# Dilated local attention and a mixer MLP on one core: the last q/k channels placed by DMA, three blocks turned by DMA, and a new order of all operations

## The chip, the core and the metric

The kernel runs on one core of a Trainium2 chip. The core has five engines that run side by side and meet only at semaphores: PE (matrix multiply, with PEld for its weight loads), DVE (vector), ACT (scalar functions), POOL (general purpose) and SP, which here only issues DMA transfers. Sixteen DMA engines carry them. PE writes its results to PSUM, eight banks of 128 x 512 float32; PE's operands lie in SBUF, 128 partitions wide. The metric is the device time of one execution in microseconds (us), the median of three runs.

## The reference

The input x has 2048 rows of 448 values (bf16). A layer of attention is followed by a mixer and an MLP, each with a residual:

```python
h  = x + A(layernorm(x))            # A: 16 heads of 28, then @ wo
h2 = h + B(layernorm(h))
# A: every query sees 8 keys, at its own row and 2, 4, ... 14 rows before it
off = jnp.arange(8) * 2
logits = einsum("bhsd,bhswd->bhsw", q, k[rows - off]) * 28**-0.5   # masked above the first row
o = einsum("bhsw,bhswd->bhsd", softmax(logits), v[rows - off])
# B: first half mixes rows, second half is an MLP
g  = gelu(layernorm(x) @ w1)        # four groups of 112 channels, moved by +1, -1, +2, -2 rows
x1 = x + moved(g) @ w2
out = x1 + gelu(layernorm(x1) @ w3) @ w4    # 448 -> 1792 -> 448
```

## The kernel before

The rows are worked in four blocks of 512 (block 0 to 3), each of four tiles of 128 rows, through these phases; the names stand in the prediction too.

- N1: statistics of x (DVE) and its normalization, per tile, into `lntm`. A1: the normalized rows are turned so that channels lie on partitions (`transposed`, into `actT`), then the q and k products on PE, in groups of 128 channels: q0, k0, q1, k1, q2, k2, and one group q3k3 of the 64 channels left of each. Each group is copied out of its PSUM bank by ACT or DVE.
- The group q3k3 comes as two half blocks X and Y, with q in partitions 0 to 63 and k in 64 to 127. Four copies of 64x256 put them in place (`qT[..., 3, ...]` and `kr[t]`), and small copies (the halos) fill the 16 rows before each stretch of keys that the attention reaches back to; `kk` holds the other keys, with a halo of its own.
- V: the v product, copied to `vt`; transfers vwp, vwa, vwb and vwc spread `vt` into windows of 80 rows (`vw`).
- A2: attention's logits. DVE multiplies the queries with all eight shifted keys (`qk_r`; qk c0 to c2 are 4096 wide, qk c3 is the half group and 2048 wide), and PE sums over the channels of a head (L c0 to c3). S: the softmax (max, sub, Exp, sum, Ln, Exp, product into `pb`), and its turn on PE, copied out by ACT (pt).
- A3: DVE spreads the weights (bd), PE multiplies them with the windows of v (AV), and ACT or DVE copies the result (aT). O: the product with wo and the residual, which gives h in `xin` (xin sum).
- B1: statistics and normalization of h, a DMA turn, and M: the product with w1, Gelu on ACT into `gT`. Three of the four groups need a second Gelu into moved columns.

The second half runs over five units of 2, 4, 4, 4 and 2 tiles. B2: the mix (the product with w2 of the moved columns; mix2,3 is the pair of tiles 2 and 3) and its residual on DVE (xb); T: normalization and a DMA turn; W3: fourteen groups with w3 and their Gelus; B3: the product with w4, the last sum on DVE (ost) and the store.

A product of two groups is done by `duo`: two matmuls run at a time, one in the upper and one in the lower 64 rows of the array; it has a first and a second half (A and B) that can stand apart in the order.

Nothing of the order is found at run time. `S.add` and `S.group` note every operation with what it reads and writes, numbered as they are made. `ORDER` is a list of these numbers, written out, that gives one sequence for all engines; each engine takes its own operations from it in that order, and waits with semaphores for the others. `arrange` gives out PSUM banks and other buffers along the sequence. `OTHER` lists operations that go to their second engine (mostly ACT to DVE). All DMAs are issued by SP, in the order of the list: a transfer whose data isn't ready holds up all that stand behind it.

`TURN` says for each phase and block how rows are turned: "t" by PE (32 transposes of 64x64 in four groups, two PSUM banks and two copies), "d" by one DMA. `NORM` gives the engine that normalizes ("a": ACT by default, DVE where `OTHER` says so; this needs the negated mean times the inverse deviation, a small operation `nmr` on DVE), `STATS` and `POWER` who makes sums and powers.

Of the kernel before, what the change touches and what calls it, by code (L numbers as in the profile page):

```python
# [5 lines left out]
ACT = mybir.ActivationFunctionType  # L6
# [6 lines left out]
TURN = {'A1': 'tttt', 'B1': 'dddd', 'B2': 'ddddd'}  # L13
NORM = {'N0': 'vvvv', 'N1': 'avvv', 'B1': 'avvv', 'B2': 'avvvv'}
STATS = {'N1': 'vvva', 'B1': 'avaa', 'B2': 'avvvv'}
NBD, NLN, NACT, NSM, NO = 3, 2, 4, 1, 3
POWER = {'N1': 'aaaa', 'B1': 'aaaa', 'B2': 'apapp'}
RESIDUAL = 'ttvv'
ORDER = """
# [30 lines left out]
"""  # L50
OTHER = """
104 127 196 197 199 402 408 411 519 525 528 582 583
# [79 lines left out]
class _Sched:  # L132
# [59 lines left out]
    def arrange(self, sequence, other=()):  # L192
# [4 lines left out]
        done = set()  # L197
        self.gorder = []
        for n, k in enumerate(sequence):
# [3 lines left out]
            op.deps |= op.sdeps  # L203
            for d in op.deps | op.odeps:
                if d not in done:
                    raise RuntimeError("operation %d (%s) stands before %d (%s)" % (k, op.tag, d.idx, d.tag))
# [68 lines left out]
def bass_sequential_preLN__sliding_local_dilated__mixer_s_mlp__prompt_kernel(  # L275
# [25 lines left out]
    A_W4 = A_W + 4 * (1344 + 128)  # L301
    A_QG = A_W4 + NF * 448
# [6 lines left out]
    with ExitStack() as es:  # L309
# [17 lines left out]
        st6 = sb("st6", [128, 8, 6], F32)  # L327
        mv = sb("mv", [128, 3, NTL, 2], F32)
# [20 lines left out]
        P_h3 = _Pool("h3", lambda k: h3T[:, k, :], NF + 2)  # L349
        P_st = _Pool("st", lambda k: st6[:, k, :], 8)  # L350
# [70 lines left out]
        def load_x(i, n):  # L421
            return dma("x%d" % i, xin[:, i:i + n, :], xv[:, i:i + n, :], 128 * n * D * 2)

        def load_rows(chan, dst, src, lo, n):

            for h in range(2):
                dma("%s%s" % (chan, "ab"[h]), dst[:, 2 * h:2 * h + 2, :], src[192 * h:192 * h + 256, lo:lo + n].rearrange("(c k) n -> k c n", k=128), 256 * n * 2)
# [21 lines left out]
        w4_v = B_w4.rearrange("(f k) n -> k f n", k=128)  # L449
        for f in range(0, NF, 7):  # L450
            dma("w4%d" % f, w4_s[:, f:f + 7, :], w4_v[:, f:f + 7, :], 128 * 7 * D * 2)
        for eng in ("sp", "pool", "act"):
            loads = [op for op in S.ops if op.tag == "load" and op.eng == eng]
            for a, b in zip(loads, loads[1:]):
                b.odeps.add(a)
# [164 lines left out]
        def setup_late(after):  # L620
# [18 lines left out]
            late("memset", ap=vw[0:PADK, 0, 0, :], constant=0.0)  # L639
            late("memset", ap=gT[:, :, 0:2], constant=0.0)  # L640
# [31 lines left out]
        def phase_A1(t):  # L672
# [31 lines left out]
            for h, b in enumerate((X, Y)):  # L704
                copy(qT[64 * h:64 * h + 64, 3, now:now + 256], b(lambda v: v[0:64, 0:256]))
                copy(kr[t][64 * h:64 * h + 64, :, PADK:], b(lambda v: v[64:128, 0:256].rearrange("p (j n) -> p j n", j=4)), False)
            copy(kr[t][64:128, :, 0:PADK], last(X, 0, 4), False)
            copy(kr[t][0:64, 1:4, 0:PADK], last(Y, 0, 3), False)
            if t + 1 < NST:
                copy(kr[t + 1][0:64, 0:1, 0:PADK], last(Y, 3, 1), False)  # L710
                copy(kk[t + 1][:, :, 0:PADK], kk[t][:, :, 512:KVW])

        def phase_V(t):
# [3 lines left out]
            def group(il, upper):  # L717
                b = _Tile(P_bank)
                return sums(lambda lo, n: b(lambda v: v[:, 0:D]), lambda c, part: a(lambda v: v[part, il, c, :]),
                            lambda c, part, lo, n: wqkv_s[part, c, 2 * D:3 * D], upper), \  # L720
                    lambda: copy(vt[:, sl, il, :].rearrange("p (h n) -> p h n", n=32)[:, :, 0:DH], b(lambda v: v[:, 0:D].rearrange("p (h n) -> p h n", n=DH)))
# [12 lines left out]
        def phase_A2(t):  # L734
# [34 lines left out]
            S.add("dve", "tensor_tensor", alts=[("pool", [("tensor_tensor", mult)])], **mult)  # L769
# [57 lines left out]
        def phase_B1(t):  # L827
# [14 lines left out]
            def group(g, upper):  # L842
                b = _Tile(P_bank)
                def evict():
                    act(gT[:, g, 2 + t * 512:2 + (t + 1) * 512], b(), ACT.Gelu_apprx_tanh)
                    if g in MOVED:
                        lo, m, early = MOVED[g]
                        at = 2 + t * 512 - early
                        skip = max(0, -at)
                        act(gT[lo:lo + m, g, at + skip:at + 512], b(lambda v: v[lo:lo + m, skip:]), ACT.Gelu_apprx_tanh)  # L850
                        if t == NST - 1:
                            dve("memset", ap=gT[lo:lo + m, g, at + 512:at + 512 + early], constant=0.0)

                return sums(lambda lo, n: b(halves(lambda v: v)), lambda c, part: w1_s[part, c, g * 128:(g + 1) * 128],
                            lambda c, part, lo, n: rows(a, c, 0, 4, part), upper), evict
# [9 lines left out]

        def phase_B2(u):
# [162 lines left out]
```

## Time and profile before

| what | value |
|---|---|
| median of 3 runs | 193.51 us (193.17 to 193.54) |
| the profiled execution | 193.18 us, its span 191.7 us |
| PE busy | 181.3 us, 95% of the span |
| ACT busy | 132.9 us, 69% |
| DVE busy | 129.5 us, 68% |
| POOL busy | 29.3 us, 15% |
| granted clock of PE | 0.999 |
| DMA | 17.03 MB, mean 89 GB/s |

The span goes from the program's first instruction to its last; the execution's own time is some 1.5 us longer. "Busy" counts instructions that run or stand in the engine's pipeline, as a union, so neighbours that overlap count once. A row of the profile gives line, engine and operation, what it writes and what it reads (`ps` is PSUM; `arena` holds most weights, q, k, the mixer's groups and the second half's sums), shapes as partitions x elements, the count, then busy time and the mean of one in ns, then the engine's idle time before them and what ended it. All rows have line 987, where every operation is issued; so they are told apart by what they write and read. A row of the order of time gives start, length, engine, what, and in brackets the idle time before it. SPq rows are issues of DMAs; "to landing" is from issue to the arrival of the data.

### The profile page before, as it was taken

The page shows a single profiled execution, that of the slowest core. Times are in us where ns is not written, and L with a number is a line of the kernel's source. Part 1 is how long each engine was busy: PE and PEld are TensorE (multiplying, and loading weights), DVE is VectorE, ACT ScalarE, POOL GpSimd, SP SyncE. Part 2 cuts the span into 40 slices and gives each one's busy share as a digit, 9 for nine tenths or more (in the row PEclk, how much of TensorE's full clock was granted, in tenths as well). Part 3 has the DMA queues.
Part 4 walks back from the last instruction along what each step waited for, and adds up shares of the span by engine and source line. Part 5 has one row for each costly group of instructions (what it writes and reads, how often), then busy time and mean ns, then how long its engine had stood idle before and what let it go on. Part 6 is the DMA issues. An engine that isn't in the chain of part 4 may idle for free.

```text
span 191.7 us, 5740 instructions
## 1 busy us (share of the span) xinstructions
PE 181.3 (95%) x2482; PEld 92.6 (48%) x2482; DVE 129.5 (68%) x229; ACT 132.9 (69%) x310; POOL 29.3 (15%) x63
## 2 busy tenths in 40 slices
PE   6999999999999868989999999999999999999994
PEld 2584533453444333347545444455444544555672
DVE  7799999999999999899876960036988022002203
ACT  4579999999999999999594998860148004821340
POOL 3240000000004000202076000022077600000000
PEclk9999999999999999999999999999999999999999
DMA  5999791004604179480805024006100812000111
GB/s 144 349 268 186 190 320 36 10 3 118 149 3 85 28 64 262 140 178 5 109 3 113 2 50 87 0 3 146 36 27 0 164 51 72 0 3 0 51 48 48
DMA packets 30272, 17.03 MB, mean 89 GB/s; under 512 B 18936, under 2 KB 29736, under 8 KB 30248
## 3 DMA queue, kind: packets, MB, share of 16 engines
q1 hardware_dynamic: 30248, 16.68, 36.7%
q8 instruction: 19, 0.31, 0.7%
q14 instruction: 5, 0.04, 0.1%
HBM read 8.04 MB, written 1.84 MB: 51 GB/s over the span
## 4 chain that ended last, share of the span: by engine, by line
PE 66%; ACT 21%; DVE 5%; DMA 2%; POOL 1%; issue 1%; SPq 1%; POOLq 0%; ACTq 0%
PE ps L987 66%; ACT arena L987 7%; ACT lntm L987 4%; ACT actT L987 2%; DMA vw<-vt 2%; ACT vt L987 2%; ACT L982 1%; DVE lntm L987 1%; DVE st L987 1%; SPq L987 1%; ACT xin L987 1%; ACT ls L987 1%; ACT L987 1%; DVE bd_r L987 1%; DVE actT L987 1%
## 5 line engine op out<-in xcount | busy, mean ns | idle before, releaser
L987 PE MATMUL ps<-actT,arena 64*128 64x256 bf16 (+1 forms) x756 | 68.8, 329 | 1.3 <-DVE arena L987 0.7
L987 ACT ACTIVATE h3T<-ps 128x512 bf16<-128x512 f32 (+1 forms) x70 | 30.3, 525 | 39.3 <-PE ps L987 39.2
L987 PEld LDWEIGHTS ps<-actT,arena 64*128 64x128 bf16 x756 | 35.5, 94 | 30.7 <-PE ps L987 2.1
L987 PE MATMUL ps<-arena,h3T 64*128 64x448 bf16 (+2 forms) x434 | 44.4, 344 | 0.0
L987 ACT ACTIVATE arena<-ps 128x512 bf16<-128x512 f32 (+10 forms) x86 | 40.1, 515 | 3.5 <-PE ps L987 2.8
L987 DVE SCALAR_TENSOR_TENSOR ost<-ps,mrs,arena 128x448 bf16<-128x448 f32 (+1 forms) x17 | 10.6, 652 | 36.4 <-PE ps L987 36.4
L987 DVE TENSOR_TENSOR qk_r<-arena 128x4096 bf16<-128x4096 bf16 (+1 forms) x16 | 32.0, 2017 | 0.7 <-PE ps L987 0.5
L987 PEld LDWEIGHTS ps<-arena,h3T 64*128 64x128 bf16 (+1 forms) x434 | 23.0, 94 | 18.7 <-issue 0.2
L987 POOL TENSOR_TENSOR arena<-arena,xin 128x448 f32<-128x448 f32 x16 | 17.2, 1091 | 45.3 <-DVE lntm L987 45.3
L987 DVE TENSOR_TENSOR bd_r<-arena,bmask 80x2048 bf16<-80x2048 bf16 x16 | 18.9, 1213 | 0.9 <-PE ps L987 0.7
L987 ACT ACTIVATE actT<-ps 128x512 bf16<-128x512 f32 (+2 forms) x21 | 14.6, 743 | 2.1 <-PE ps L987 2.1
L987 PE MATMUL ps<-wo_s,actT 64*128 64x448 bf16 x128 | 14.3, 351 | 0.6 <-DVE actT L987 0.4
L987 PE MATMUL ps<-actT,w_s 64*128 64x512 bf16 x112 | 13.3, 377 | 1.5 <-ACT rs_y L987 0.7
L987 PE MATMUL ps<-arena,actT 64*128 64x448 bf16 x112 | 12.4, 350 | 0.4 <-ACT vt L987 0.4
L987 PE MATMUL ps<-w_s,arena 64*128 64x448 bf16 x112 | 11.6, 350 | 0.9 <-ACT arena L987 0.7
L987 ACT ACTIVATE lntm<-xin,nm 128x448 bf16<-128x448 bf16 x16 | 10.5, 661 | 2.6 <-DVE nm L987 2.6
L987 DVE SCALAR_TENSOR_TENSOR arena<-xin,rs_y,ps 128x448 f32<-128x448 bf16 x16 | 10.3, 672 | 2.1 <-PE ps L987 2.0
L987 DVE TENSOR_SCALAR lntm<-arena,mv,rs_y 128x512 bf16<-128x512 f32 x14 | 10.2, 774 | 2.1 <-POOL rs_y L987 2.0
L987 POOL TENSOR_TENSOR pb<-ls,mx 128x512 bf16<-128x512 f32 x2 | 3.3, 1640 | 52.6 <-ACT mx L987 52.6
L987 DVE BATCH_NORM_STATS2 st<-xin 128x6 f32<-128x448 bf16 x16 | 9.4, 614 | 0.8 <-DMA xin<-in_A_x_dram 0.8
L987 PEld LDWEIGHTS ps<-actT,w_s 64*128 64x128 bf16 x112 | 5.2, 94 | 8.6 <-PE ps L987 1.7
L987 PEld LDWEIGHTS ps<-wo_s,actT 64*128 64x128 bf16 x128 | 5.6, 94 | 7.2 <-PE ps L987 1.4
(73 smaller groups left out, 161.9 us busy)
## 6 DMA issues: line engine op xcount, KB each, us to landing
arena<-in_B_w_dram SPq DMA_DIRECT2D x2, 896.0 KB, 6.7
out_dram<-ost SPq DMA_DIRECT2D x15, 112.0 KB, 1.8
arena<-in_B_w_dram SPq DMA_DIRECT2D x2, 784.0 KB, 5.7
vw<-vt SPq DMA_DIRECT2D x4, 320.0 KB, 4.3
vw<-vt SPq DMA_DIRECT2D x4, 256.0 KB, 4.3
arena<-in_A_wqkv_dram SPq DMA_DIRECT2D x2, 448.0 KB, 5.0
xin<-in_A_x_dram SPq DMA_DIRECT2D x2, 448.0 KB, 7.5
xin<-in_A_x_dram SPq DMA_DIRECT2D x3, 224.0 KB, 5.6
```

The lines of the kernel that those rows point to most:

```text
L982: eng.preload_act_table_set("natural_log_exp_and_others")
L987: inst = getattr(eng, meth)(**kw)
```

## The change

- Blocks 1 to 3 of A1 are turned by one DMA each (`TURN['A1']` becomes "tddd"); block 0 stays on PE.
- q3k3: X and Y are each copied whole (128x256) into a stage with one buffer (`stg`), and small DMAs on SP put the parts in place: sq and sk for each half (64 partitions x 512 bytes), kra, krb and krc for the halos of `kr` and kkc for that of `kk` (runs of 32 bytes).
- `NORM` names ACT as the default for N1 and B1 of all blocks and for units 0 and 1; `OTHER` sends most of these to DVE. The product into `pb` is always DVE's.
- w4 takes the place of w_qkv in `arena`, so its two loads are made after V3; they were among the first loads.
- Five output buffers in place of three. Options that stay off (`COPIED`, `ALONE`).
- `ORDER` and `OTHER` are new. In the new sequence, ahead of L c3 of block 3, PE has all it had there before except the twelve turns, and also mix2,3 (both halves) and the first half of mix4,5. The loads of w3 stand between the DMA turns of B1's block 1 and of unit 0, where they were among V0's transfers; those of wo, w1 and w2 stand between the stages' parts of blocks 2 and 3 and block 3's vw transfers.

```diff
-TURN = {'A1': 'tttt', 'B1': 'dddd', 'B2': 'ddddd'}
-NORM = {'N0': 'vvvv', 'N1': 'avvv', 'B1': 'avvv', 'B2': 'avvvv'}
+TURN = {'A1': 'tddd', 'B1': 'dddd', 'B2': 'ddddd'}
+NORM = {'N0': 'vvvv', 'N1': 'aaaa', 'B1': 'aaaa', 'B2': 'aavvv'}
-NBD, NLN, NACT, NSM, NO = 3, 2, 4, 1, 3
+NBD, NLN, NACT, NSM, NO = 3, 2, 4, 1, 5
...
+HALO = 'dddd'
+STAGE = 'dddd'
+COPIED = ()
+ALONE = False
 ORDER = """
...
-    A_W4 = A_W + 4 * (1344 + 128)
-    A_QG = A_W4 + NF * 448
+    A_W4 = A_W
+    A_QG = A_W4 + max(NF * 448, 4 * (1344 + 128))
...
+        stg = sb("stg", [128, 1, 2, 256], BF16)
...
+        P_sg = _Pool("sg", lambda k: stg[:, k, :, :], 1)
...
-            for h, b in enumerate((X, Y)):
-                copy(qT[64 * h:64 * h + 64, 3, now:now + 256], b(lambda v: v[0:64, 0:256]))
-                copy(kr[t][64 * h:64 * h + 64, :, PADK:], b(lambda v: v[64:128, 0:256].rearrange("p (j n) -> p j n", j=4)), False)
-            copy(kr[t][64:128, :, 0:PADK], last(X, 0, 4), False)
-            copy(kr[t][0:64, 1:4, 0:PADK], last(Y, 0, 3), False)
-            if t + 1 < NST:
-                copy(kr[t + 1][0:64, 0:1, 0:PADK], last(Y, 3, 1), False)
-                copy(kk[t + 1][:, :, 0:PADK], kk[t][:, :, 512:KVW])
+            if STAGE[t] == "d":
+                stage = _Tile(P_sg)
+                for h, b in enumerate((X, Y)):
+                    copy(stage(lambda v, h=h: v[:, h, :]), b(lambda v: v[:, 0:256]))
+                for h in range(2):
+                    dma("sq%d%d" % (t, h), qT[64 * h:64 * h + 64, 3, now:now + 256], stage(lambda v, h=h: v[0:64, h, :]), 64 * 512)
+                    dma("sk%d%d" % (t, h), kr[t][64 * h:64 * h + 64, :, PADK:], stage(lambda v, h=h: v[64:128, h, :].rearrange("p (j n) -> p j n", j=4)), 64 * 512)
...
+            if HALO[t] == "d":
...
+                dma("kra%d" % t, kr[t][64:128, :, 0:PADK], end(0, 0, 4), 64 * 4 * PADK * 2)
+                dma("krb%d" % t, kr[t][0:64, 1:4, 0:PADK], end(1, 0, 3), 64 * 3 * PADK * 2)
+                if t + 1 < NST:
+                    dma("krc%d" % t, kr[t + 1][0:64, 0:1, 0:PADK], end(1, 3, 1), 64 * PADK * 2)
+                    dma("kkc%d" % t, kk[t + 1][:, :, 0:PADK], kk[t][:, :, 512:KVW], 128 * 3 * PADK * 2)
...
-            S.add("dve", "tensor_tensor", alts=[("pool", [("tensor_tensor", mult)])], **mult)
+            dve("tensor_tensor", **mult)
...
+        def load_w4():
+            last = S.ops[-1]
+            w4_v = B_w4.rearrange("(f k) n -> k f n", k=128)
+            for f in range(0, NF, 7):
+                dma("w4%d" % f, w4_s[:, f:f + 7, :], w4_v[:, f:f + 7, :], 128 * 7 * D * 2).odeps.add(last)
...
+                    if S.tag == "V%d" % (NST - 1):
+                        S.tag = "w4"
+                        load_w4()
```

More of the change, by code (lines that the diff above doesn't have):

```diff
@@ L203, in arrange @@
             op.deps |= op.sdeps
+            if not ALONE:
+                pass
+            elif op.insts[0][0] == "dma_start_transpose":
+                op.deps.update(turned + moved)
+                turned, moved = [op], []
+            elif op.is_dma and not callable(op.chan):
+                op.deps.update(turned)
+                moved.append(op)
             for d in op.deps | op.odeps:
@@ L327, in bass_sequential_preLN__sliding_local_dilated__mixer_s_mlp__prompt_kernel @@
         st6 = sb("st6", [128, 8, 6], F32)
+        stg = sb("stg", [128, 1, 2, 256], BF16)
+        gM = sb("gM", [128, max(1, len(COPIED)), QGW], BF16) if COPIED else None
         mv = sb("mv", [128, 3, NTL, 2], F32)
@@ L448, in bass_sequential_preLN__sliding_local_dilated__mixer_s_mlp__prompt_kernel @@
         load_rows("w3", w3_s, B_w3, 0, F)
[L449 to L455, printed above, removed]
+        loads = [op for op in S.ops if op.is_dma]
+        for a, b in zip(loads, loads[1:]):
+            b.odeps.add(a)
         TOP, BOT = slice(0, 64), slice(64, 128)
@@ L639, in setup_late @@
             late("memset", ap=vw[0:PADK, 0, 0, :], constant=0.0)
+            if COPIED:
+                late("memset", ap=gM[64:128, :, 0:2], constant=0.0)
+                late("memset", ap=gM[64:128, :, 2 + SEQ:4 + SEQ], constant=0.0)
             late("memset", ap=gT[:, :, 0:2], constant=0.0)
@@ new lines, in phase_A1 @@
+            if HALO[t] == "d":
+                if STAGE[t] == "d":
+                    end = lambda h, lo, n: stage(lambda v: v[64:128, h, :].rearrange("p (j n) -> p j n", j=4)[:, lo:lo + n, 64 - PADK:])
+                else:
+                    end = lambda h, lo, n: kr[t][64 * h:64 * h + 64, lo:lo + n, 64:]
+                dma("kra%d" % t, kr[t][64:128, :, 0:PADK], end(0, 0, 4), 64 * 4 * PADK * 2)
[3 more added lines that the diff above has]
+                    dma("kkc%d" % t, kk[t + 1][:, :, 0:PADK], kk[t][:, :, 512:KVW], 128 * 3 * PADK * 2)
+            else:
+                copy(kr[t][64:128, :, 0:PADK], last(X, 0, 4), False)
+                copy(kr[t][0:64, 1:4, 0:PADK], last(Y, 0, 3), False)
+                if t + 1 < NST:
+                    copy(kr[t + 1][0:64, 0:1, 0:PADK], last(Y, 3, 1), False)
+                    copy(kk[t + 1][:, :, 0:PADK], kk[t][:, :, 512:KVW])
@@ L718, in group @@
                 b = _Tile(P_bank)
-                return sums(lambda lo, n: b(lambda v: v[:, 0:D]), lambda c, part: a(lambda v: v[part, il, c, :]),
-                            lambda c, part, lo, n: wqkv_s[part, c, 2 * D:3 * D], upper), \
+                return sums(lambda lo, n: b(lambda v: v[:, lo:lo + n]), lambda c, part: a(lambda v: v[part, il, c, :]),
+                            lambda c, part, lo, n: wqkv_s[part, c, 2 * D + lo:2 * D + lo + n], upper), \
                     lambda: copy(vt[:, sl, il, :].rearrange("p (h n) -> p h n", n=32)[:, :, 0:DH], b(lambda v: v[:, 0:D].rearrange("p (h n) -> p h n", n=DH)))
@@ L847, in evict @@
                         lo, m, early = MOVED[g]
-                        at = 2 + t * 512 - early
+                        now = 2 + t * 512
+                        at = now - early
                         skip = max(0, -at)
-                        act(gT[lo:lo + m, g, at + skip:at + 512], b(lambda v: v[lo:lo + m, skip:]), ACT.Gelu_apprx_tanh)
+                        to = gM if g in COPIED else gT
+                        if g in COPIED:
+                            dma("gm%d%d" % (t, g), gM[lo:lo + m, g, at + skip:at + 512], gT[lo:lo + m, g, now + skip:now + 512], m * 1024)
+                            rest = slice(64, lo) if lo > 64 else slice(lo + m, 128)
+                            dma("gn%d%d" % (t, g), gM[rest, g, now:now + 512], gT[rest, g, now:now + 512], (64 - m) * 1024)
+                        else:
+                            act(gT[lo:lo + m, g, at + skip:at + 512], b(lambda v: v[lo:lo + m, skip:]), ACT.Gelu_apprx_tanh)
                         if t == NST - 1:
-                            dve("memset", ap=gT[lo:lo + m, g, at + 512:at + 512 + early], constant=0.0)
-                return sums(lambda lo, n: b(halves(lambda v: v)), lambda c, part: w1_s[part, c, g * 128:(g + 1) * 128],
-                            lambda c, part, lo, n: rows(a, c, 0, 4, part), upper), evict
+                            dve("memset", ap=to[lo:lo + m, g, at + 512:at + 512 + early], constant=0.0)
+                return sums(lambda lo, n: b(halves(lambda v: v[:, lo:lo + n], n // 128)), lambda c, part: w1_s[part, c, g * 128:(g + 1) * 128],
+                            lambda c, part, lo, n: rows(a, c, lo // 128, n // 128, part), upper), evict
             for g in (0, 2):
@@ L874, in side @@
                     part = (TOP, BOT)[h]
-                    return [(gT[part, c, 2 + i * 128 + SHIFT[c, h]:130 + i * 128 + SHIFT[c, h]], (lambda lo, m, c=c: w2_s[part, c, lo:lo + m])) for c in range(n)]
+                    return [((gM if h and c in COPIED else gT)[part, c, 2 + i * 128 + SHIFT[c, h]:130 + i * 128 + SHIFT[c, h]], (lambda lo, m, c=c: w2_s[part, c, lo:lo + m])) for c in range(n)]
                 def out():
@@ L910, in group @@
                 b = _Tile(P_bank)
-                return sums(lambda lo, m: b(halves(lambda v: v[:, 0:128 * n], n)), lambda c, part: w3_s[part, c, f * 128:(f + 1) * 128],
-                            lambda c, part, lo, m: rows(a, c, 0, n, part), upper), \
+                return sums(lambda lo, m: b(halves(lambda v: v[:, lo:lo + m], m // 128)), lambda c, part: w3_s[part, c, f * 128:(f + 1) * 128],
+                            lambda c, part, lo, m: rows(a, c, lo // 128, m // 128, part), upper), \
                     lambda: act(h3[u][f](lambda v: v[:, 0:128 * n]), b(lambda v: v[:, 0:128 * n]), ACT.Gelu_apprx_tanh)
```

16 lines of the change are left out of this document (11 added, 5 removed), and 60 rows, old and new, of the table ORDER.

## The prediction, made before the change was run

> **What bounds the kernel now.** I read the page's busy shares, then the busy time by stage, then PE's order of time where it idles, and last what the DMA queue issues.
>
> ```profile
> PE 181.3 (95%) x2482; PEld 92.6 (48%) x2482; DVE 129.5 (68%) x229; ACT 132.9 (69%) x310; POOL 29.3 (15%) x63
> ```
>
> ```profile
> 10.00:30.00 20.00, 20.00 (x301) 10.85 (x299) 19.45 (x33) 19.32 (x51) 1.97 (x18) 1.00 0.94 231
> 30.00:60.00 30.00, 29.30 (x584) 13.61 (x582) 29.93 (x34) 29.79 (x81) 0.00 (x1) 1.00 0.20 46
> 60.00:75.00 15.00, 11.69 (x242) 5.34 (x240) 14.76 (x25) 14.68 (x32) 2.20 (x1) 1.00 0.60 100
> 75.00:90.00 15.00, 13.98 (x180) 6.95 (x178) 14.13 (x33) 14.62 (x37) 2.56 (x4) 1.00 0.51 143
> 90.00:101.00 11.00, 10.57 (x234) 5.79 (x232) 9.13 (x14) 8.78 (x19) 3.45 (x4) 1.00 0.37 51
> 110.00:189.00 79.00, 78.88 (x818) 41.56 (x814) 27.12 (x60) 34.98 (x71) 12.81 (x14) 1.00 0.19 46
> ```
>
> The columns are window, length, then PE, PEld, DVE, ACT and POOL busy, the granted clock, DMA share and GB/s. From 10 to 75 us PE, DVE and ACT are all full: DVE misses 0.55 + 0.07 + 0.24 us, ACT about the same. After 110 us only PE is. So what counts is the work that PE still has ahead of it when the attention stage lets it go, and when that is. The clock is full throughout. PE's idle time is in the middle:
>
> ```profile
> 63.54 3.67 PE L987 MATMUL ps<-actT,w_s 64*128 64x512 bf16 x28 [0.70 <-ACT rs_y L987]
> 68.01 0.42 PE L987 MATMUL ps<-bd_r,vw 80*32 80x64 bf16 x32 [0.45 <-DVE lntm L987]
> 69.07 0.42 PE L987 MATMUL ps<-bd_r,vw 80*32 80x64 bf16 x32 [0.65 <-ACT arena L987]
> 70.17 1.74 PE L987 MATMUL ps<-w_s,arena 64*128 64x448 bf16 x14 [0.68 <-ACT arena L987]
> 74.52 3.43 PE L987 MATMUL ps<-actT,w_s 64*128 64x512 bf16 x28 [0.65 <-ACT rs_x L987]
> ...
> 80.70 0.40 PE L987 MATMUL ps<-qk_r,zc 128*32 128x512 bf16 x4
> 81.17 3.06 PE L987 MATMUL ps<-w_s,arena 64*128 64x448 bf16 x28
> 84.07 1.04 PE L987 MATMUL ps<-actT,arena 64*128 64x256 bf16 x16
> 85.82 2.59 PE L987 MATMUL ps<-actT,arena 64*128 64x256 bf16 x40 [0.71 <-DVE arena L987]
> ```
>
> M0's wait (63.54) and M1's (74.52) are put down to ACT's powers, but ACT had been done with those; a DMA turn is the other input, and a turn takes this long:
>
> ```profile
> 59.08 11.46 SPq L987 DMA_TRANSPOSE actT<-lntm  x2
> actT<-lntm SPq DMA_TRANSPOSE x9, 4.3
> DMA to landing us min/median/max: 3.1/4.3/5.6
> ```
>
> Issued at 59.08, a median turn lands at 63.4, and M0 starts at 63.54.
>
> **The marker.** I use the last logit sum of block 3 (L c3), the four matmuls at 80.70. Behind it PE runs until the last output tile, after 101 us almost without a pause. It needs DVE's last q-k product (qk c3):
>
> ```profile
> 78.55 1.23 DVE L987 TENSOR_TENSOR qk_r<-arena 128x2048 bf16<-128x2048 bf16 x1 [0.45 <-PE ps L987]
> ```
>
> which ends at 79.78.
>
> **The change, part by part: PE.** Twelve groups of transposes go, four for each of blocks 1 to 3. Block 1's hold PE from 13.93 to 14.39, so 0.46 us each block, 1.4 in all:
>
> ```profile
> 13.93 0.63 PE L987 MATMUL ps<-ident,lntm 64*128 64x64 bf16 x32
> 14.39 2.81 PE L987 MATMUL ps<-arena,actT 64*128 64x448 bf16 x28
> ```
>
> Counting the new sequence up to L c3 of block 3, PE has the same groups ahead of it as before, less those twelve, plus three half groups of unit 1's mix: mix2,3 whole and the first half of mix4,5, 22 of the 28 matmuls at 81.17. Those 28 last until 84.07, so 22/28 x 2.90 = 2.3 us; less a share of the small wait among them, 2.2. So behind the marker PE has 2.2 us less to do; the 1.4 us lies ahead of it, where PE isn't the only full engine. That is the gain if the marker stays in its place.
>
> **ACT.** Going: six evictions of PE's turns, fifteen copies of 64x256, the halo copies.
>
> ```profile
> L987 ACT ACTIVATE actT<-ps 128x1024 bf16<-128x1024 bf16 x6 | 6.2, 1077 | 0.0
> L987 ACT ACTIVATE arena<-ps 64x256 bf16<-64x256 f32 x15 | 5.6, 376 | 2.3 <-PE ps L987 2.1
> L987 ACT ACTIVATE h3T<-ps 128x256 bf16<-128x256 f32 x28 | 8.6, 406 | 11.1 <-PE ps L987 11.0
> L987 ACT ACTIVATE lntm<-xin,nmr,rs_y 128x512 bf16<-128x512 bf16 x1 | 0.8, 803 | 0.0
> ```
>
> Without the small halo copies that is 11.8 us. Coming: eight copies of 128x256 to the stage, at the nearest row's 406 ns 3.2 us, and six more normalizations at 803 ns, 4.8 us. ACT gets at least 3.8 us lighter. By the sequence it changes its table twelve times, as before.
>
> **DVE** decides when the marker comes. Ahead of qk c3 of block 3 the new sequence has, against the old: two xin sums more, one S2 product that POOL did, two xb normalizations, one vt copy, eight small mean or shift operations, one actT copy; and five x normalizations, two aT copies and one q copy fewer.
>
> ```profile
> L987 DVE SCALAR_TENSOR_TENSOR xin<-ps,xin 128x448 bf16<-128x448 f32 x8 | 4.7, 622 | 1.8 <-PE ps L987 1.5
> L987 DVE TENSOR_TENSOR pb<-ls,mx 128x512 bf16<-128x512 f32 x2 | 1.4, 683 | 0.0
> L987 DVE TENSOR_SCALAR lntm<-arena,nm,rs_y 128x512 bf16<-128x512 f32 x2 | 1.0, 542 | 0.0
> L987 DVE TENSOR_SCALAR nm<-mv 128x4 f32<-128x4 f32 x5 | 0.8, 165 | 0.1
> L987 DVE TENSOR_SCALAR lntm<-xin,mv,rs_y 128x448 bf16<-128x448 bf16 x12 | 4.0, 388 | 0.3 <-ACT rs_y L987 0.3
> L987 DVE CAST actT<-ps 128x512 bf16<-128x512 f32 x4 | 2.7, 682 | 0.0
> ...
> 83.72 0.68 DVE L987 SCALAR_TENSOR_TENSOR arena<-xin,rs_y,ps 128x448 f32<-128x448 bf16 x1
> ...
> 85.10 1.26 DVE L987 SCALAR_TENSOR_TENSOR arena<-xin,rs_y,ps 128x448 f32<-128x448 bf16 x2
> ```
>
> With 0.68 for the vt copy and 0.4 for the actT and q copies that is 1.24 + 0.68 + 1.08 + 0.68 + 1.32 + 0.4 - 1.94 - 1.36 - 0.4 = 1.7 us by the means. Neighbours overlap by some 0.1 (one takes 0.68, two 1.26), and there are seven more, so the net is about 1.1. DVE is no lighter. It can win back its idle time between 10 us and qk c3, 0.86 + 0.45 = 1.3 us, part of which was waiting for ACT and PE. Marker: earliest 79.78 + 1.1 - 1.3 = 79.6, latest 79.78 + 1.1 + 1.3 = 82.2 if as much idle time comes on top. I take half won back, 80.2, and 0.5 for new hand-overs: 80.7, where it was (PE was 0.9 behind DVE there, and now follows at once).
>
> **POOL** loses the two products (the first took 2.2 us); nobody waits for its other work. **The start** is untouched: the first real matmul waits for the second q/k weight half, and the first five loads are issued in the same order. The shared place of w4 and w_qkv, the fifth output buffer and the unused options add nothing to an engine; w4 now waits for V3, and stands on the queue behind a vw transfer of block 3. It takes 5.7 us (next rows), from about 81 until 87, and is needed near 88: hidden, with 1 us to spare.
>
> **The queue (SP)** gets 33 more issues (3 turns, 16 stage parts, 14 halos), all in the attention stage.
>
> ```profile
> 9.95 8.40 SPq L987 DMA_DIRECT2D w_s<-in_B_w_dram  x11
> 43.16 5.36 SPq L987 DMA_DIRECT2D vw<-vt  x6
> 48.55 0.54 ACT L987 ACTIVATE xin<-ps 128x448 bf16<-128x448 f32 x1
> arena<-in_B_w_dram SPq DMA_DIRECT2D x2, 784.0 KB, 5.7
> vw<-vt SPq DMA_DIRECT2D x4, 320.0 KB, 4.3
> vw<-vt SPq DMA_DIRECT2D x4, 48.0 KB, 3.6
> ```
>
> One issue costs 0.76 (8.40/11) to 0.89 us (5.36/6) in a row of waiting ones; a stage part lands within about 3.6 us. The stage has one buffer, so ACT's next stage copy waits for all parts of the block before, with every later eviction behind it; blocks follow at some 10 us, so I cost that at nothing, and if that cover goes, it costs up to 3.6 us a block. q3/k3 are read only by qk c3, the last product of its block, which hides their flight. The x turns of blocks 1 to 3 add 4.3 us between a normalization and q/k; other groups of V, O and L cover it, except perhaps in block 1, which is ahead of the marker.
>
> **Waits behind the marker.** Before: 0.71 (W3 at 85.82), 0.43 in 90 to 101, small ones 0.3: 1.4. After: W3 of unit 0 follows mix4,5's last half, 0.6 us behind the marker's product, and its turn is issued three DVE instructions ahead of qk c3: at a median landing 0.4 late, at 5.6 us 1.7 late, at 3.1 not at all. W3's evictions stand behind the gelu table again: 0.8. O3 and unit 1's turn: 0.5 each. I take 2.2; ends 0.6 and 5.
>
> **Sum.** 2.2 less to do, 0.8 more waiting, marker unmoved: 1.4 us off. The profiled execution took 193.18 us (span 191.7), 0.33 under the median; from the median, 193.51 - 1.4 = 192.1.
>
> **Rivals.**
> 1. DVE wins back nearly all its idle time (marker 79.7, 1.0 earlier) and PE waits only 1.0 behind it: 2.2 + 1.0 + 0.4 = 3.6, so 189.9. For it: ACT is lighter, and most of PE's waits at 63 to 75 were for ACT or a turn. Against it: DVE has 1.1 more.
> 2. Nothing comes of it: the marker slips 1.5 to 82.2, 2.2 - 0.8 - 1.5, so 193.6. For it: the stage part and the turn put two queue trips between PE and DVE.
> 3. Slower: the queue runs in order, and between the parts of block 3's stage X and B1's turn of block 0 stand fourteen issues. Stage X follows block 0's residual sums on ACT, which end at 49.1 now (48.55 + 0.54). At 0.65 each the turn goes out at 58, about when its rows are ready; at 0.89 at 61.5, and M0 comes 3.4 later. Two weight loads of the mixer and the next turn stand behind it. The next gelus, mix and xb sums on DVE slip with it, about 2.7 us at the marker: 193.51 - 1.4 + 2.7 = 194.8. It decides from about 0.8 us per issue on. Against it: these parts are small. The Trainium skill, "DMA: Bandwidth & Descriptors", Rules for kernel authors, speaks against the change here: many small transfers should be joined, since under 64 KB one pays mostly overhead. The 48 KB row agrees, 3.6 us against 4.3 for 320 KB. By that rule, an estimate, splitting costs a whole trip's overhead each time, and the time is this rival's.
>
> **How the numbers follow.** Forecast 0.42 (190.8 to 193.0), rival 1 0.20, rival 2 0.13, rival 3 0.25. A difference under 0.2% (0.39 us) can't be told from none. Faster: forecast and rival 1, 0.62; same: rival 2, 0.13; slower: 0.25. The range leaves out the far tails of rivals 1 and 3: 189.2 to 195.5.
>
> **What would show it.** Right: qk c3 of block 3 ends between 80 and 81.5, L c3 follows at once, DVE is over 97% busy from 10 to 80, PE has no 32-matmul row of turns, and the last matmul ends near 187.5. Wrong towards rival 1: the marker before 80. Towards rival 3: gaps under 0.1 us between SP's issues from 49 to 60, a first B1 turn after 60, PE idle over 1.5 us before M0. What breaks the argument: DVE idle for over 2 us waiting for stage parts, or w4 landing after W3 of unit 0 is done.

## The result, and the profile after

The changed kernel took 199.56 us (median of four executions, 197.57 to 200.34) against 193.52 for the kernel before beside it: ratio 1.0293, 95% interval 1.0249 to 1.0338. The prediction was 192.1 with a range of 189.2 to 195.5, so it was wrong, and on the wrong side. The profiled execution is the shortest of the four, 197.57, span 195.8; the four go with the granted clock of their whole span (0.991 for 197.57 and 199.05, 0.983 for 200.06 and 200.34), which is part of the answer.

From the page of the kernel after: the busy shares, and the granted clock in 40 slices of 4.9 us.

```profile
PE 181.3 (93%) x2386; PEld 95.0 (49%) x2386; DVE 129.8 (66%) x234; ACT 128.7 (66%) x289; POOL 28.2 (14%) x61
PEclk9999999997999999999999999999999999999999
```

PE is as busy as before with 96 matmuls fewer: some ran slower. ACT lost 4.2 us, DVE nothing. Busy time by stage, in the columns of the prediction's table:

```profile
10.00:30.00 20.00, 19.15 (x231) 9.88 (x227) 18.59 (x30) 18.33 (x45) 2.17 (x19) 1.00 0.60 117
30.00:60.00 30.00, 27.15 (x529) 12.89 (x526) 26.00 (x30) 23.69 (x63) 0.00 (x0) 0.94 0.50 109
60.00:75.00 15.00, 11.81 (x256) 5.12 (x245) 13.82 (x25) 13.90 (x30) 0.00 (x0) 1.00 0.75 135
75.00:90.00 15.00, 13.28 (x146) 5.41 (x144) 14.73 (x27) 13.55 (x30) 3.01 (x1) 1.00 0.51 168
```

The second row differs most: from 30 to 60 us DVE is busy for 26.0 us instead of 29.9, PE for 27.2 instead of 29.3, and the clock is 0.94. PE's order of time there (start, length, what, and the idle time before it):

```profile
41.88 0.42 PE L1038 MATMUL ps<-bd_r,vw 80*32 80x64 bf16 x32
44.87 0.93 PE L1038 MATMUL ps<-wo_s,actT 64*128 64x448 bf16 x8 [2.57 <-DMA wo_s<-in_A_wo_dram]
...
46.05 1.59 PE L1038 MATMUL ps<-wo_s,actT 64*128 64x448 bf16 x8
...
47.80 1.70 PE L1038 MATMUL ps<-wo_s,actT 64*128 64x448 bf16 x8
...
49.64 0.46 PE L1038 MATMUL ps<-ident,pb 64*80 64x64 bf16 x16
50.27 0.92 PE L1038 MATMUL ps<-wo_s,actT 64*128 64x448 bf16 x8
```

O01 of block 0 waits 2.57 us for wo. Then the same eight matmuls take 0.93, 1.59, 1.70 and 0.92: two halves ran at little over half speed. The granted clock says the same (here and in the hardware section, steps of 3.41 us, PE's busy time behind the length, the clock third from the end):

```profile
42.77:46.18 3.41, 1.25 (x12) 0.52 (x14) 3.41 (x3) 1.62 (x5) 0.00 (x0) 1.00 0.60 161
46.18:49.60 3.42, 3.42 (x20) 1.43 (x18) 1.24 (x1) 1.16 (x4) 0.00 (x0) 0.50 0.73 158
```

The turn of `pb`, whose product DVE had ready at 45.2, stands behind them at 49.64. DVE runs dry for it (its next work needs the turned weights, which ACT copies out):

```profile
45.14 2.28 DVE L1038 TENSOR_TENSOR qk_r<-arena 128x4096 bf16<-128x4096 bf16 x1
50.77 1.22 DVE L1038 TENSOR_TENSOR bd_r<-arena,bmask 80x2048 bf16<-80x2048 bf16 x1 [3.35 <-ACT arena L1038]
```

Why wo is late is in SP's order. The kernel before issued wo from 7.2 to 9.9 us; now its four loads go out from 34.12 to 43.1, behind a DMA turn and parts of block 2's stage:

```profile
34.12 0.62 SPq L1038 DMA_DIRECT2D wo_s<-in_A_wo_dram  x1
34.86 1.79 SPq L1038 DMA_TRANSPOSE actT<-lntm  x1
36.70 3.18 SPq L1038 DMA_DIRECT2D arena<-stg  x4
39.92 2.05 SPq L1038 DMA_DIRECT2D wo_s<-in_A_wo_dram  x2
42.01 0.49 SPq L1038 DMA_DIRECT2D arena<-stg  x1
42.54 0.57 SPq L1038 DMA_DIRECT2D wo_s<-in_A_wo_dram  x1
```

A second place is M0: B1's turn of block 0 goes out at 62.58, 1.4 after its rows are normalized (61.15), and PE waits for it (one row of SP, one of PE):

```profile
62.58 3.13 SPq L1038 DMA_TRANSPOSE actT<-lntm  x1
```

```profile
67.22 1.93 PE L1038 MATMUL ps<-actT,w_s 64*128 64x512 bf16 x14 [1.51 <-DMA actT<-lntm]
```

The marker (L c3 of block 3, 80.70 before) follows DVE's product at once, but at 86.85, 6.15 later:

```profile
86.85 0.40 PE L1038 MATMUL ps<-qk_r,zc 128*32 128x512 bf16 x4 [0.40 <-DVE qk_r L1038]
```

PE's last matmul ends at 193.28 instead of 188.88. From the marker to there it is 106.4 us instead of 108.2.

### The profile page after: what moved, and what is told of

It reads as the page before. It is cut to its first block, busy times and chain, and to the rows that moved or that the text cites. A ratio compares the mean times of both kernels' runs of the same rounds, so it can differ in the third digit from the quotient of the medians.

```text
span 195.8 us, 5589 instructions
## 1 busy us (share of the span) xinstructions
PE 181.3 (93%) x2386; PEld 95.0 (49%) x2386; DVE 129.8 (66%) x234; ACT 128.7 (66%) x289; POOL 28.2 (14%) x61
## 4 chain that ended last, share of the span: by engine, by line
PE 64%; DVE 12%; DMA 9%; ACT 9%; SPq 3%; issue 1%; DVEq 0%; ACTq 0%
PE ps L1038 64%; DMA actT<-lntm 5%; DVE qk_r L1038 5%; SPq L1038 3%; ACT lntm L1038 3%; DVE st L1038 2%; ACT arena L1038 2%; DMA arena<-stg 2%; DVE lntm L1038 2%; DMA wo_s<-in_A_wo_dram 1%; DVE xin L1038 1%; DMA xin<-in_A_x_dram 1%; DVE arena L1038 1%; ACT L1038 1%; ACT L1033 1%
## 5 line engine op out<-in xcount | busy, mean ns | idle before, releaser
L1038 PE MATMUL ps<-actT,arena 64*128 64x512 bf16 (+1 forms) x756 | 68.5, 329 | 2.0 <-DMA actT<-lntm 0.6
L1038 PEld LDWEIGHTS ps<-actT,arena 64*128 64x128 bf16 x756 | 38.0, 94 | 29.2 <-DMA actT<-lntm 1.5
L1038 PE MATMUL ps<-arena,h3T 64*128 64x448 bf16 (+2 forms) x434 | 45.5, 343 | 0.1
L1038 ACT ACTIVATE arena<-ps 128x512 bf16<-128x512 f32 (+7 forms) x60 | 33.5, 593 | 3.6 <-PE ps L1038 3.1
L1038 PEld LDWEIGHTS ps<-arena,h3T 64*128 64x128 bf16 (+1 forms) x434 | 24.7, 94 | 17.6 <-PE ps L1038 0.5
L1038 POOL TENSOR_TENSOR arena<-arena,xin 128x448 f32<-128x448 f32 x16 | 19.5, 1243 | 92.1 <-DVE lntm L1038 92.1
L1038 PE MATMUL ps<-wo_s,actT 64*128 64x448 bf16 x128 | 16.3, 377 | 2.8 <-DMA wo_s<-in_A_wo_dram 2.6
L1038 DVE TENSOR_SCALAR lntm<-arena,mv,rs_y 128x512 bf16<-128x512 f32 x13 | 8.8, 705 | 3.0 <-ACT rs_y L1038 2.1
L1038 ACT ACTIVATE actT<-ps 128x512 bf16<-128x512 f32 (+1 forms) x16 | 9.1, 596 | 1.3 <-PE ps L1038 1.1
L1038 PE MATMUL ps<-qk_r,zc 128*32 128x512 bf16 x112 | 8.6, 384 | 0.6 <-DVE qk_r L1038 0.4
```

What stands on the lines that cost most here:

```text
L1038: inst = getattr(eng, meth)(**kw)
```

## The experiments

Theory A: transfers stand too late in SP's one order, wo above all; the pause this makes on PE also lowers its clock. Theory B: the stage's one buffer and small transfers hold up the stage. Theory C: DVE bounds it in any case. Numbers in `ORDER` are operations: 18 is the load of x tiles 8 to 11, 19 of 12 to 15, 20 to 23 wo, 24 to 29 w1, 30 to 34 w2, 385 V2's vwb. In each, ratios are against the kernel before run beside it.

**wo early.**

```diff
-18 ... 19 ... 20 ... 21 22 ... 23
+18 19 20 21 22 23 ...
```

> After, with the last x load and the four wo loads issued behind the load of x tiles 8 to 11 (near 6.3 us); all else in its order. Theory A (the wo loads stand too late in SP's order): O01 A of block 0 starts near 42.3 instead of 44.87, PE's 2.57 us wait and the two slow halves of O0 (1.96 and 2.00 instead of 1.11) go, L c3 of block 3 comes about 4.4 earlier, 194 to 195.5 us against 199.56. Theory B (the stage's one buffer and its small transfers hold the stage up): the wait is only taken over by the next late part, 198.5 to 200. Theory C (DVE bounds the stage in any case): L c3 of block 3 moves by less than 1 us, 198.5 to 200.

195.74 us, ratio 1.0076 (1.0038 to 1.0115). O01 A starts at 42.76 without a pause. By the ratios about three quarters of the loss went with this edit (it also moves one x load, 19, forward): the time is just above A's range, and below what B and C allow. But the marker came at 85.83, only 1.0 earlier: PE now paused 2.18 us before M0, and the clock fell there (PE, then the stretch from 65 to 70 us, clock in the third last column):

```profile
64.78 2.46 PE L1038 MATMUL ps<-actT,w_s 64*128 64x512 bf16 x14 [2.18 <-DMA actT<-lntm]
```

```profile
65.00:70.00 5.00, 4.87 (x58) 1.57 (x56) 4.86 (x9) 2.42 (x5) 0.00 (x0) 0.66 0.71 168
```

The ten executions fall apart by their clock: four at 1.0 took 193.78 to 194.22, six at 0.982 to 0.991 took 195.72 to 196.28.

**w1 and w2 early as well.**

```diff
-385 ... 24 ... 25 26 ... 27 28 ... 29 ... 30 31 32 ... 33 34
+23 24 25 26 27 28 29 ...
+385 30 31 32 33 34 ...
```

> As the kernel with wo early, and also w1's six loads behind wo (near 8.7 us) and w2's five behind V2's vwb (48.3 us), where SP idled 4.5 us. Theory A: five issues fewer between block 3's stage parts and B1's turn of block 0, which goes out as soon as the rows are normalized; M0's 1.5 us wait falls to about 0.5 and the time is 0.7 to 1.2 below that of wo early: 193 to 194.5. Theory B: as wo early within 0.4. The wait before M0 itself tells whether issues of the queue or DVE's normalizations set the turn.

195.82, ratio 1.0126 (1.0072 to 1.018): a miss. Block 1's x turn landed at 19.50 instead of 17.78. It was issued at 14.36 instead of 13.41, behind the loads, and took 5.14 us instead of 4.37 beside them: 0.95 of the delay is the queue, 0.77 the longer flight. PE paused 1.66 before 19.55, the clock fell there (a 6 among the slices), and DVE idled 3.5 us before block 0's qk c3. M0's wait fell from wo early's 2.18 to 1.53, not to 0.5. More is not better: the loads delay a DMA turn, by their place and by their traffic.

**PE kept busy before O0.** wo stays late; ten matmuls of no use fill the pause.

```diff
+                if t == 0 and il == 0:
+                    mms([(b(), ident[:], bass.AP(ident, 0, [[128, 128], [0, 4], [1, 128]]), True, True, 512, None)] * 10)
```

> After, and ahead of O01 A of block 0 ten matmuls of ident by ident, 512 columns, into O01's own bank (overwritten by it; some 2.3 us more of work for PE), so that PE does not stand still while wo is on its way. wo stays late. Theory of the clock (the pause of 2.57 us makes the granted clock drop): O01 A still starts near 44.9, but O01 B and O23 A take 1.1 each, and the time falls by 1.3 to 1.8 although PE has more to do: about 197.9. Rival (the two slow halves have another cause, such as DMA traffic): they stay at 2.0, and the time is that of after within 0.5.

196.24, ratio 1.0145 (1.0099 to 1.019), every execution at a clock of 1.0. PE:

```profile
42.85 2.33 PE L1039 MATMUL ps<-ident 128*128 128x512 bf16 x10
45.78 0.93 PE L1039 MATMUL ps<-wo_s,actT 64*128 64x448 bf16 x8 [0.59 <-DMA wo_s<-in_A_wo_dram]
46.97 0.93 PE L1039 MATMUL ps<-wo_s,actT 64*128 64x448 bf16 x8
47.92 0.92 PE L1039 MATMUL ps<-wo_s,actT 64*128 64x448 bf16 x8
```

O01 starts 0.9 us later than in the change, PE does 2.3 us more, and the kernel is 3.3 us faster: the slow halves are the clock's, and the clock cost more than the pause. The gain is larger than the 1.3 to 1.8 expected, which had only counted the profiled execution's slow halves; the median of the change is 2 us above that one.

**The kernel before, with only wo's last load late.**

```diff
+        S.ops[23].deps.add(S.ops[172])
-19 20 21 ... 22 23 24
+19 20 21 ... 22 24 ... 23 177
```

(172 is AV 2 of block 0, 177 is O01 A.)

> The kernel before, with the last of the four wo loads issued only when AV 2 of block 0 is done (43.1 us); nothing else of the change. Theory A with the clock: O01 A waits until 45.5 to 46 (2.4 to 2.9 us), the next halves run slow, and the kernel takes 196.5 to 198, as much as the whole change cost at this place. Without a fall of the clock: at most 2.6 more, 195 to 196. Theory B (stage parts needed for the harm): under 1 us more.

199.85, ratio 1.0291 (1.0237 to 1.0345): one late load of 98 KB costs as much as the whole change, with none of the change's other parts. That the two ratios are equal is chance: the pause is longer here, 3.09 us against 2.57. PE, then two stretches:

```profile
46.56 1.67 PE L988 MATMUL ps<-wo_s,actT 64*128 64x448 bf16 x8 [3.09 <-DMA wo_s<-in_A_wo_dram]
...
76.48 3.04 PE L988 MATMUL ps<-w_s,arena 64*128 64x448 bf16 x14 [0.68 <-ACT arena L988]
```

```profile
42.00:48.00 6.00, 2.91 (x90) 1.33 (x78) 6.00 (x5) 5.18 (x15) 0.00 (x0) 0.81 0.29 71
48.00:54.00 6.00, 5.86 (x42) 1.84 (x38) 0.41 (x1) 0.82 (x3) 0.00 (x0) 0.62 0.67 156
```

DVE stands still nearly all of the second stretch. It came out above the 196.5 to 198 expected: the clock was low through three halves, not two, and it fell once more at 76.5, where the fourteen matmuls of a mix took 3.04 us instead of 1.74. Between the two falls no pause of PE was longer than 0.71.

**wo, w1 and w2 issued by POOL**, behind its setup, all else as in the change.

```diff
-            dma("wo%d" % j, wo_s[32 * j:32 * j + DH, :, :], wo_v[j], DH * D * 8)
+            dma("wo%d" % j, wo_s[32 * j:32 * j + DH, :, :], wo_v[j], DH * D * 8, "pool")
```

> After, with the loads of wo, w1 and w2 issued by POOL (idle from 13 to 75 us) behind its setup, near 13 us; nothing else moved, so SP has 15 issues fewer in the attention stage. Theory A (the transfers added to SP's order are late because of what stands ahead of them): O01 A of block 0 starts near 42.3, B1's turn of block 0 goes out within 0.3 us of its last normalization (58.2 with wo early, where it went out at 59.35), M0's wait falls from 2.25 to about 1.1, the granted clock stays full there, L c3 of block 3 comes at 82.5 to 83.5 and the time is 192.5 to 194. Rival (the turn's own flight, not the queue, delays M0): M0's wait stays at 2 or more and the time near that of wo early, 195 to 196.

198.2, ratio 1.0226 (1.0175 to 1.0278): a miss. Block 1's x turn, issued at 13.53 as in the change (13.41), landed at 21.78 instead of 17.78 beside fifteen loads, and PE paused 3.77, with a fall of the clock:

```profile
21.82 3.71 PE L1039 MATMUL ps<-actT,arena 64*128 64x512 bf16 x18 [3.77 <-DMA actT<-lntm]
```

At M0 SP was free for 2.6 us before it issued the turn, yet that turn took 5.94 us to land instead of 4.60. So the queue was not all of M0's wait; the rival has a share.

**On top of that, three of DVE's operations given to ACT** (vt1 of block 3 and the two normalizations of unit 0 leave `OTHER`: 494, 583, 584).

> As w on pool, and three operations ahead of the last q-k product go from DVE to ACT: vt1 of block 3 and the normalizations of the two mixer tiles of unit 0 (0.6 + 0.5 + 0.5 to 1.2 us of DVE). Theory (DVE is full there and its added work, not PE's, sets L c3 of block 3): 1 to 2 us faster than w on pool, 191.5 to 192.8. Rival (PE or ACT sets it by then): within 0.5 of w on pool, or slower, because ACT's Gelus wait behind these.

199.86, ratio 1.0302 (1.0261 to 1.0343), slower by 1.7 than its base: the rival. From L c3 to W3 it is 2.19 us instead of 0.91: unit 0's turn waits for the normalizations, now behind Gelus on ACT. The rest may be the clock, which in the profiled execution was low at 20 us for 6.8 us instead of 3.4.

```profile
91.01 3.47 PE L1038 MATMUL ps<-actT,arena 64*128 64x256 bf16 x56 [1.12 <-DMA actT<-lntm]
```

**On top of w on pool, q3 and k3 put in place by copies again.**

```diff
-STAGE = 'dddd'
+STAGE = 'cccc'
```

> As w on pool, with q3 and k3 put in place by four ACT or DVE copies of 64x256 a block as in the kernel before, no stage and no sq/sk transfers; the halos stay transfers. SP has 16 issues fewer, the copying engines 8 copies more. Theory A (the stage's transfers cost by their place in the queue, and that is relieved by POOL): within 0.7 us of w on pool, slower rather than faster. Theory B (the one stage buffer and the small transfers' flight hold up the evictions and qk c3): faster than w on pool by 1 us or more.

201.51, ratio 1.0371 (1.0318 to 1.0424), 3.3 above its base where 0 to 0.7 was expected. Part of it may be the clock, which was low at 20 us for 6.8 us instead of 3.4; at half speed that is at most 1.7. Theory B needed a gain of 1 us or more, and falls.

**PE kept busy before M0**, with wo early: nine such matmuls in m01's bank.

```diff
+                if t == 0 and g == 0:
+                    mms([(b(), ident[:], bass.AP(ident, 0, [[128, 128], [0, 4], [1, 128]]), True, True, 512, None)] * 9)
```

> The kernel with wo early, and nine matmuls of ident by ident ahead of M0's first half of block 0, into its own bank, so that PE works while it waits there (2.25 us). The runs of wo early lie in two groups, near 194.0 with a granted clock of 1.0 and near 196.0 with 0.98 to 0.99. Theory of the clock: the pause before M0 is long enough to make the clock drop in some executions and not in others; with the fillers all runs have a clock of 1.0 and take about 194.0. Rival (the two groups have another cause): the two groups stay, median near 195.7.

193.54, ratio 0.9995 (0.9978 to 1.0013): twelve executions, all at 0.999 or 1.0. PE and the same stretch as above:

```profile
62.11 2.12 PE L1039 MATMUL ps<-ident 128*128 128x512 bf16 x9
64.34 1.92 PE L1039 MATMUL ps<-actT,w_s 64*128 64x512 bf16 x14
```

```profile
65.00:70.00 5.00, 4.27 (x152) 1.90 (x148) 5.00 (x7) 3.58 (x7) 0.00 (x0) 1.00 0.72 151
```

With wo in time and the clock held, the change costs nothing against the kernel before. L c3 comes at 83.96, 2.9 earlier than in the change, so DVE's work alone (theory C) didn't hold it at 86.85.

**w1 into SP's hole**, wo early: the last five w1 loads behind 385, where SP idled 1.2 us.

```diff
-385 ... 25 26 ... 27 28 ... 29
+385 25 26 27 28 29 ...
```

> The kernel with wo early, and the last five w1 loads moved up behind V2's vwb, into SP's idle 1.2 us before block 3's stage parts, with w1's first. B1's turn of block 0 can go out at 58.2 instead of 59.35. Theory (the queue makes that turn late): M0 starts 0.8 to 1.1 earlier than with wo early, its wait falls to 1.2 to 1.5, the clock stays full, and the time is 192.8 to 193.6. Rival (the turn's flight grows by what it gains, as it did with the loads on POOL: 5.9 instead of 5.4): M0 as with wo early, 194 to 196.

193.02. Of thirteen executions eleven kept a clock of 1.0 (192.34 to 193.64); the ratio, 0.9953 (0.9926 to 0.9981), is of these eleven, and by it the kernel is faster. The other two took 195.44 and 195.80. The turn went out at 57.98 instead of 59.35 and landed at 63.88 instead of 64.73, so 0.85 of 1.37 arrived: the queue's share, and the rest is the turn's longer flight.

**Both.**

> Both: w1 placed early and five fillers ahead of M0. By the theories of the queue and of the clock the best of all, 192.7 to 193.5, all runs at a clock of 1.0: the change's own gain behind L c3 (2.2) less the later L c3. If DVE's added work is all that is left, L c3 of block 3 stands at 82 to 83.5, 1.3 to 2.8 later than in the kernel before.

193.08, ratio 0.9985 (0.9967 to 1.0004), all twelve executions at 0.999 or 1.0; L c3 at 83.27, inside the expected 82 to 83.5. Against the eleven executions of w1 placed that is no gain: the fillers hold the clock, and do nothing else.

**The mix behind the marker again**, on w1 placed:

```diff
-624 625 632 511 626 629 512 513 514 633
+511 512 624 625 632 633 513 514 626 629
```

(624, 625 mix2,3; 632, 633 mix4,5; 511 qk c3; 512 L c3; the rest are DVE's xb and softmax.)

> As w1 placed, with one part of the new sequence undone: mix2,3 (both halves) and the first half of mix4,5 stand behind L c3 of block 3 again, and their residuals behind that. The prediction's step (2.2 us of PE's work lies ahead of the marker and is hidden by DVE there): L c3 comes no later, the stretch from it to the end is 2.2 to 2.6 us longer, and the time 1.8 to 2.5 above w1 placed. Rival (those halves delay L c3 by as much as they save behind it): within 0.6 of w1 placed.

196.56, ratio 1.0144 (1.0105 to 1.0183), 3.5 above w1 placed. From M0 to L c3 it is 19.62 us with and without (82.49 - 62.87; 83.27 - 63.65 in the kernel with both), so DVE does hide those halves ahead of the marker. But the time behind is no clean price: PE paused 3.51 before L c3, and the clock was 0.50 after it (PE, then the stretch):

```profile
82.49 0.62 PE L1038 MATMUL ps<-qk_r,zc 128*32 128x512 bf16 x4 [3.51 <-DVE qk_r L1038]
83.04 5.84 PE L1038 MATMUL ps<-w_s,arena 64*128 64x448 bf16 x28
```

```profile
83.00:88.00 5.00, 4.87 (x30) 1.45 (x28) 2.65 (x4) 4.01 (x7) 0.00 (x0) 0.50 0.92 293
```

The 28 matmuls of the mix took 5.84 instead of 3.06, so 2.8 of the 3.5 is the clock. From L c3 to PE's last matmul it is 109.7 us, against 106.5 with w1 placed and 105.6 with both. PE worked 6.06 us of it at half speed, an estimated 3.0 lost; so 0.2 to 1.0 is left as the price of the halves behind the marker, where 2.2 to 2.6 was expected. They partly fill waits that PE has there otherwise (0.3 us of idle time in place of 1.0 to 1.6).

**POOL's residual of tile xb1 moved behind that of xb4** (586 behind 650), on both.

> As the kernel with wo and w1 placed and five fillers ahead of M0 (193.08), with POOL's residual of tile xb1 moved behind that of xb4, some 15 us later on POOL. Theory (POOL's 3.0 us product slows the normalization of xb0 beside it from 0.54 to 1.26): the normalization takes 0.55, L c3 of block 3 comes 0.6 to 0.7 earlier (82.5), and the time is 192.3 to 192.6. Rival (the slow normalization has another cause, such as its operands): it stays at 1.26, and the time within 0.2 of 193.1.

192.86, ratio 0.9948 (0.9931 to 0.9965), the lowest of all, though its interval overlaps that of w1 placed. One of its six executions took 235.06 at a clock of 1.0, which nothing here explains. DVE's normalization of xb0 in the kernel with both, POOL's product beside it there, and the normalization now:

```profile
79.00 1.26 DVE L1039 TENSOR_SCALAR lntm<-arena,nm,rs_y 128x512 bf16<-128x512 f32 x1
```

```profile
76.98 3.01 POOL L1039 TENSOR_TENSOR arena<-arena,xin 128x448 f32<-128x448 f32 x1 [64.49 <-DVE lntm L1039]
```

```profile
77.99 0.54 DVE L1039 TENSOR_SCALAR lntm<-arena,nm,rs_y 128x512 bf16<-128x512 f32 x1
```

The mechanism is shown, at 0.72 us. Of the 0.5 to 0.8 expected of the time, 0.2 came by the medians and 0.7 by the ratios.

**Block 0's L c1 earlier on PE** (150 behind 229), without and with the fillers.

> As wo and w1 placed (no fillers), with the residual of xb1 late, and block 0's L c1 moved ahead on PE, behind the second q/k half of block 1. Theory (the wait of 1.08 us before block 0's qk c3 is for the q-k buffer that L c1 frees): that wait falls below 0.2, all of DVE's later work moves up by 0.6 to 0.9, and the runs at a full clock take 191.3 to 192.0. Rival (the wait is for the stage's last transfer, landed at 22.3): it stays near 1, and the time is that of the residual alone, 192.3 to 192.6.

> The same with five fillers ahead of M0: all runs at a clock of 1.0; 191.4 to 192.2 by the theory, 192.3 to 192.7 by the rival. DVE's idle time from 10 us to qk c3 of block 3 is 2.0 or less by the theory.

193.41, ratio 0.9985 (0.9962 to 1.0009), and 193.59, 0.9991 (0.9968 to 1.0014): no gain, and with the fillers 0.7 slower than without this move. The wait before block 0's qk c3 is gone, so it was for the buffer that L c1 frees, but it came back one product later (DVE):

```profile
22.81 1.22 DVE L1038 TENSOR_TENSOR qk_r<-arena 128x2048 bf16<-128x2048 bf16 x1
24.78 2.29 DVE L1038 TENSOR_TENSOR qk_r<-arena 128x4096 bf16<-128x4096 bf16 x1 [0.76 <-ACT arena L1038]
```

DVE's idle time up to block 3's qk c3 was 3.3, not 2.0.

## Why the prediction was wrong

- **The step that failed: the moved loads were not costed at all.** The change's list had them ("those of wo, w1 and w2 stand between the stages' parts"), and the prediction named w4's load and 33 more issues, but never asked when wo is first read (43.02) and when its last load would be issued. The wait was put at nothing without a reason. The runs showed 2.57 us of it at O0, and a fall of the clock behind it. Undoing it (with one x load) takes the ratio from 1.0293 to 1.0076; doing it alone to the kernel before gives 1.0291.
- **The clock was not foreseen.** "The clock is full throughout" was true of the trace of before, whose longest pause of PE in the middle was 0.71. It isn't true of most executions of that kernel: of 72 run beside the experiments, 50 had a mean clock of 0.991 or less. Nor was PE full from 60 to 75 us, as the prediction read its table: it was busy for 11.69 of 15. The prediction priced a pause at its length. Filling the pause at O0 alone brought 3.3 us by the medians (2.9 by the ratios), at M0 2.2 (1.6).
- **The marker, 80.7 with 82.2 as the latest, came at 86.85.** Ahead of qk c3, DVE's idle time from 10 us was 6.8 instead of 1.3, where half of 1.3 was to be won back; 3.35 and 0.62 of it stand behind O0. Its work (the end of qk c3 less all idle time ahead of it) grew from 76.05 to 78.32, by 2.3 instead of 1.1: the means' 1.7 was nearer, and 0.72 is the normalization that POOL's product slows. "Nobody waits for its other work" held for POOL's results, not for DVE beside it.
- **Rival 3 had the right kind of mechanism at the wrong place.** Its fourteen issues went out at 0.69 each, under its threshold, and M0's turn was 1.4 late, with 1.51 of PE's idle time where 0.70 stood before. The larger harm of the same queue came 20 us earlier, at O0. The Trainium skill's rule that it drew on ("DMA: Bandwidth & Descriptors", Rules for kernel authors: small transfers pay mostly overhead) speaks of their size. Here the place of the loads behind them counted: with copies in place of sixteen of the small transfers the kernel was slower (1.0371 against 1.0226), part of which may be the clock.
- **Right: behind the marker.** 106.4 us instead of 108.2, 1.8 less, where 2.2 less work and 0.8 more waiting gave 1.4. By PE's busy time it was 1.9 less work (104.9 against 106.8) and 0.2 more waiting (1.6 against 1.4): the wait of 2.2 was mis-sized. L c3 followed DVE's product at once, and from M0 to L c3 the moved halves cost nothing. ACT got 4.2 lighter ("at least 3.8"). The forecast's 192.1 was nearly there once wo, w1 and POOL's product were moved and PE was kept busy: 192.86, with L c3 at 81.8. That is another kernel than the one forecast, so it doesn't save the forecast.
- What it named as breaking the argument, DVE idle for over 2 us waiting for stage parts, did not happen as named: DVE was idle for 3.35 us at once, but for O0's sake.

Not settled: why a B1 turn of block 0 takes 4.4 to 5.9 us to land when little else is on the queue, what the copies' 3.3 us consist of, what the halves of the mix are worth ahead of the marker, and where the clock falls in the kernel before.

## What to carry over

When an order is changed, list for every transfer its first reader and its place in the issuing queue, weight loads too; one load 3 us late cost 6. A pause of PE can cost more than its length, because the clock may fall behind it: here it did behind all of 2.57 us and more, and behind shorter ones, from 1.58, in some executions. So a wait that can't be removed may be worth filling with matmuls of no use. And loads moved early aren't free either: fifteen beside a DMA turn lengthened it by 4 us.

## What was unexpected of the hardware

In the profiled executions the granted clock fell to 0.50 after pauses of PE of 1.58 us (w1 placed), 1.66, 2.18, 2.57, 3.09, 3.38, 3.51, 3.77 and 3.83. It did not after 1.51 (the change, before M0), 1.64 (the mix behind), 1.68 (block 0's L c1 earlier) and 1.87 (O0 filled). And it fell at 76.47 in the kernel before with wo's last load late, after three pauses of 0.43 to 0.68. So the length of one pause does not decide it. Every time, the clock stayed low for 3.41 us or twice that.

In each trace the changes of the clock up to the last matmul lie whole steps of 3.41 us apart (in the change it rises first at 5.22 and falls at 46.19, twelve steps later). Cut into these steps, fourteen of the traces show the same (the other two have no change of the clock to count from): in the step ahead of each of the ten falls PE was busy for 0.36 to 1.68 us, less than half; a step with 1.69 us or more kept a full clock. While it was low, steps of 1.86 to 2.72 us kept it low, and 3.33 and more raised it. The rows with the result show such a pair, 1.25 us busy and then 0.50; this is the step ahead of the fall at 76.47, the one nearest to the limit:

```profile
73.05:76.47 3.42, 1.68 (x102) 0.92 (x97) 3.42 (x7) 3.32 (x8) 0.00 (x0) 1.00 0.02 4
```

A pause of some 2 us therefore lowers the clock or doesn't, by where it lies against the steps. That would account for the two of thirteen executions (w1 placed) and six of ten (wo early), though only one execution of each has a trace. One step at half clock is 1.7 us of some 192, a mean clock of 0.991. In the kernel before's own trace the emptiest such step has 2.12 us busy, from 68.52 to 71.93; where the clock falls in its 50 executions at 0.991 or less, no trace shows.

The Trainium skill ("TensorE: Matmul & The Clock Gate", Part 1 and Why this matters for your kernels) states a free-running window of 3.4 us and warns of idle gaps over about 3 us. The steps of 3.41 us agree with the window. The gap of 3 us does not: half a step idle was enough here, in one pause of 1.58 us or in several, and the measurement decides.

A POOL product of 128x448 float32 took 3.01 us beside DVE's work, and DVE's normalization after it 1.26 instead of 0.54. That agrees with "GPSIMD Engine Reference", Specifications, in the Trainium skill, by which the two share their ports to SBUF.
